# Gated MLP weights prepared during attention, one step per group, on one Trainium2 core

## The chip, the cores and the metric

The kernel runs on one core of a Trainium2 chip. The metric is the time of one execution on the device in microseconds (us), as the median of several runs. The core has a matrix engine (TensorE, PE in the rows; its weight loads are PEld), a vector engine (VectorE, DVE), a scalar engine (ScalarE, ACT), a general engine (GpSimd, POOL), an engine that issues the transfers here (SyncE, SP), and 16 DMA engines. The engines run their own instruction queues in order and wait for one another through semaphores.

## What is computed

Three layers follow one another: attention with pooled queries, a gated MLP with a spatial gate, and a mixer with a low-rank token part and a channel MLP.

```python
# 1 attention: q, k, v are (4, 8, 1152, 64)
q_pool = q.reshape(B, H, S // 2, 2, D).mean(axis=3)
attn = softmax(scale * q_pool @ k^T)          # 576 x 1152 for each of 32 heads
x = (attn @ v), heads side by side            # (4, 576, 512)
# 2 gated MLP
h = relu(x @ w_in);  u, v = halves of h       # w_in 512 x 1024
v_n = (v - mean) / sqrt(var + 1e-6)
gated = u * (w_spatial @ v_n + b_spatial)     # w_spatial 576 x 576
x = gated @ w_out                             # w_out 512 x 512
# 3 mixer
u = x + (x^T @ U @ V)^T                       # U 576 x 32, V 32 x 576
out = u + relu(u @ w_ch1) @ w_ch2
```

The weights w_in, w_out, U, V, w_ch1 and w_ch2 arrive as 64-bit floats; w_spatial, q, k, v arrive as 32-bit floats.

## The kernel before

**Attention** (`attention`) works on 16 pairs of heads, j = 0 to 15. Each pair has two halves of its 576 queries (256 and 320 wide, u = 2j and 2j + 1) and nine chunks of 128 keys, so 18 chunks a pair and 288 in all. Two chunks make a group: nine groups a pair (r = 0 to 8), 144 in all. In a group TensorE first runs up to two pieces (`piece`, a 128 x 384 block of scores whose row maximum VectorE reduces from PSUM, lines 138 and 142), then the two score products and the subtraction of the maxima (`scores`, `less`); ScalarE takes the exponentials (`expo`, line 197) into tiles `pt`; GpSimd adds up the exponentials (line 202); then come up to two more pieces and the products with v of the group before (`pv`). Pieces have two PSUM buffers (`ring`), so a piece waits for VectorE's reduction of the piece two earlier. In four of the nine groups of a pair VectorE also takes half a reciprocal (line 234, `waiting`).

**Weights** (class `Weights`): the 32-bit high and low parts that the matrix products use are made from each weight block (a unit) in seven phases, each one tick apart. For a 64-bit unit: phase 0, two ScalarE activations on the loaded words (lines 431, 432); phase 1 and phase 2, one VectorE instruction each (436, 438); phase 3, a GpSimd integer add (440); phase 4, VectorE (442); phase 5, the high part, by ScalarE or VectorE (452); phase 6, the low part, by GpSimd or VectorE (457). A 32-bit unit (w_spatial) has phases 5 and 6 alone. `tick` starts a unit when the one before it is at least two ticks old, and runs the due phase of up to four begun units. Loads go through three rooms `raw`; SyncE issues the next load when a room is free. The gated MLP has 21 units: 8 of w_in, 5 of w_spatial, 4 of w_out, 2 of U, 2 of V.

**The order of the gated MLP** (`gated_mlp`) is a generator that attention resumes through `also`. In the last two pairs (j = 14 and 15) attention resumes it after each chunk, and the table `TICKS` makes 13 ticks there; only the w_in units are loaded by then. The strings in `LEFT` interleave, at the end of attention, ticks (w), the split of batch 0's x (x) and batch 0's first products with w_in (v). Then the string `START` sets the order for batch 0: D finishes v (relu, statistics), n normalises, U makes the u half, b the bias, X splits batch 1's x, G the spatial gate, P the v products of batch 1, and w is a tick. The other 13 units are loaded and prepared in these ticks. After `START` come `y_part` (products with w_out), `u_pass` and `v_pass`, and then the batches 1 to 3 in a fixed loop without weight steps except for the channel MLP's in the last batch. The channel MLP (`channel_mlp`) follows.

Each engine's queue holds the instructions in the order in which this Python code issues them (`manual_schedule`).

Of the kernel before, what the change touches and what calls it, by code (L numbers as in the profile page):

```python
# [22 lines left out]
def f(ap):  # L23
    return ap.bitcast(F32)
# [3 lines left out]

LEFT = ("x x x x w x x v x x x v v w v", "v v v w v v w v v v v w", "v v v v w v v v w")


def attention(tc, idf, q, k, v, xs, also):

# [28 lines left out]
    with ExitStack() as ctx, ExitStack() as sco:  # L62
        pt_p = ctx.enter_context(tc.tile_pool(name="pt_p", bufs=12))
        ld2 = ctx.enter_context(tc.tile_pool(name="ld2", bufs=2))
# [10 lines left out]
        first = ld.tile([128, 128], F32R, name="first", bufs=1)  # L75
# [34 lines left out]
        def round_q(j, c0=0, c1=T):  # L110
            s = st[j]
            if "qr" not in s:
                s["qr"] = ld.tile([128, T], F32R, tag="qr", name="qr")
            nc.scalar.copy(s["qr"][:, c0:c1], s["q"][:, c0:c1])

        def round_k(j, c0=0, c1=S):
            s = st[j]
            if "kr" not in s:
                s["kr"] = ld.tile([128, S], F32R, tag="kr", name="kr")
            nc.scalar.copy(s["kr"][:, c0:c1], s["k"][:, c0:c1])  # L120
# [140 lines left out]
        pool_q(1, nc.gpsimd)  # L261
        ticks = [0]
        to_rows(0)
# [5 lines left out]
        for i, group in enumerate(groups):  # L269
# [36 lines left out]
            for u, n in waiting:  # L306
# [40 lines left out]
class Weights:  # L347
# [5 lines left out]
    def __init__(self, nc, stages, most=1 << 30, keep=None):  # L353
# [7 lines left out]
        self.time = self.begun = self.loaded = self.staged = 0  # L361

    def load(self, units=(), raws=()):

# [97 lines left out]
def gated_mlp(tc, idf, w_in, w_sp, b_sp, w_out, wU, wV, xs, us, last, soon, then):  # L462
# [4 lines left out]


    nc = tc.nc
    DM, DFF = w_in.shape  # L470
# [14 lines left out]

    right, mid, banks = ExitStack(), ExitStack(), ExitStack()
    ep = room(right, "ep", side="right")
    xn = ep.tile([128, KD, T], F32, name="xn")
    xnt = ep.tile([128, KD, TAIL], F32, name="xnt")

    wi = [None, ep.tile([128, 2, KD, FF], F32R, name="wi1")]
    raws = [ep.tile([128, 1024], F32, name=f"raw{i}") for i in range(3)]
# [18 lines left out]
    def load_x(b):  # L511
        nc.sync.dma_start(out=xn, in_=xs[b].rearrange("(k p) t -> p k t", p=128))
        if b % 2 == 0:
            nc.sync.dma_start(out=xnt, in_=xs[b + 1][:, 128 * (NT - 1):T].rearrange("(k p) t -> p k t", p=128))

    w = Weights(nc, stages, keep=LAST)
# [11 lines left out]
    wi[0] = e2.tile([128, 2, KD, FF], F32R, name="wi0")  # L528
    ps = [room(banks, "ps", 4, side="right", space=PSUM)]
# [60 lines left out]

    lp = room(last, "lp")
# [4 lines left out]
    uu = lp.tile([128, NT, 2, 2, R], F32R, name="uu")  # L596
    vv = lp.tile([128, 2, T], F32R, name="vv")
    yh = lp.tile([128, 2, NT, DM], F32R, name="yh")
    gg = lp.tile([128, DM], F32R, name="gg")
    wst = ap.tile([128, 2, NT, T], F32R, name="wst")  # L600
    wo = ap.tile([128, 2, KF, DM], F32R, name="wo")
# [3 lines left out]
    twice = lp.tile([128, TAIL], F32R, name="twice")  # L605

    first = ExitStack()
    sp = room(first, "sp")
    sps = [sp.tile([128, T], F32, name=f"sp{t}") for t in range(NT)]
# [4 lines left out]
    ES, EW, EU, EV = [engines(x) for x in ("ES", "EW", "EU", "EV")]  # L614
    units = []
    for t in range(NT):
        n = rows[t]
        units.append(
            ([(slice(p, p + n), w_sp[128 * t:128 * t + n]) for p in range(0, 128, n)], 128, (T,))
            + parts(nc, lambda t=t: [wst[:, 0, t]], lambda t=t, n=n: [wst[0:n, 1, t]], eng=ES[t][0], copy=ES[t][1], low=n)  # L620
            + (sps[t],)
        )
    for k in range(KF):
        units.append(
            ([(slice(None), w_out[128 * k:128 * k + 128])], 128, (DM,))
            + parts(nc, lambda k=k: [wo[:, 0, k]], lambda k=k: [wo[:, 1, k]], eng=EW[k][0], copy=EW[k][1])
        )
    full = 128 * (NT - 1)
    tail = wU[full:T].rearrange("(k p) r -> p k r", k=1)
    for src, k, sl in (  # L630
        ([(slice(None), wU[0:full].rearrange("(k p) r -> p k r", p=128))], NT - 1, slice(0, NT - 1)),
        ([(slice(p, p + TAIL), tail) for p in (0, TAIL)], 1, slice(NT - 1, NT)),
    ):
        units.append(
            (src, 128, (k, R))
            + parts(
                nc, lambda sl=sl: [uu[:, sl, i, 0] for i in range(2)],
                lambda sl=sl: [uu[:, sl, i, 1] for i in range(2)],
                lambda st: st.rearrange("p (k r) -> p k r", r=R), EU[k == 1][0], EU[k == 1][1],
            )  # L640
        )
    for h in range(2):
        sl = slice(HT * h, HT * h + HT)
        units.append(
            ([(slice(R * i, R * i + R), wV[:, sl]) for i in range(128 // R)], 128, (HT,))
            + parts(nc, lambda sl=sl: [vv[:, 0, sl]], lambda sl=sl: [vv[:, 1, sl]], None, *EV[h])
        )
    load_x(1)
    w.load(units)

    nc.gpsimd.memset(nhalf, -0.5)
    nc.gpsimd.memset(f(wst[64:128, 1, NT - 1]), 0.0)
    nc.gpsimd.memset(f(vn[64:128, 0, NT - 1]), 0.0)
# [253 lines left out]
LAST = 4  # L907
MORE = 4
# [1 line left out]
TICK = eval(os.environ.get('TK','[.9]*7'))  # L910

# [158 lines left out]
def tile_kernel(ctx: ExitStack, tc: tile.TileContext, q, k, v, w_in, w_sp, b_sp, w_out, wU, wV, w1, w2, out):  # L1070
# [9 lines left out]
    with tc.manual_schedule(), ExitStack() as last:  # L1080
        gated = gated_mlp(
            tc, idf, w_in, w_sp, b_sp, w_out, wU, wV, xs, us, last,
            lambda: next(channel), lambda: next(channel),
        )
        begun = []

        def also(i):
            if begun:
                try:
                    gated.send(i)  # L1090
                except StopIteration:
                    pass
            else:
                begun.append(next(gated))

        attention(tc, idf, q, k, v, xs, also)
        also(0)
        last.close()
        for _ in channel:
            pass  # L1100
# [42 lines left out]
```

## Time and profile before

| | us |
|---|---|
| median of 3 runs | 1237.76 (1237.42 to 1238.48) |
| the profiled execution's own time | 1240.44 |
| its span, first to last instruction | 1238.7 |
| TensorE busy | 1164.4 (94%) |
| VectorE busy | 646.3 (52%) |
| GpSimd busy | 559.9 (45%) |
| ScalarE busy | 438.2 (35%) |

The profile is of one execution. A busy TensorE is not TensorE at its peak, since the ends of its matmuls are modelled. The last exponentials of attention begin at 526.49 us; batch 1's u products begin at 640.22 us; the channel MLP's steady part runs from about 846 us to the end. The mean granted clock of TensorE over the span is 0.973 of full speed.

### The profile page before, as it was taken

How to read it: one execution, taken by the hardware profiler on the slowest of the kernel's cores; microseconds unless marked ns; L12 is line 12 of the kernel's file. 1: busy time of each engine (PE TensorE's matmuls, PEld its weight loads, DVE VectorE, ACT ScalarE, POOL GpSimd, SP SyncE). 2: the span in 40 equal slices, each digit the busy share in tenths (PEclk: the TensorE clock that was granted, in tenths of full speed). 3: DMA queues.
4: the chain of work that ended last, by engine and by line, in shares of the span. 5: the costliest groups of instructions: out<-in, count | busy, mean ns of one | idle time of the engine just before them, and what ended most of it. 6: DMA issues, size and time to landing. Idle time of an engine off the chain costs nothing.

```text
span 1238.7 us, 18191 instructions
## 1 busy us (share of the span) xinstructions
PE 1164.4 (94%) x7116; PEld 917.8 (74%) x7116; DVE 646.3 (52%) x1158; ACT 438.2 (35%) x868; POOL 559.9 (45%) x458
## 2 busy tenths in 40 slices
PE   7999999999999999887679999889999999999998
PEld 5666666666666665567569898768999999999997
DVE  4666666666666668865433332879862212121211
ACT  2444444444444445434233333646431111111110
POOL 2777777777777777953533343634420000000000
PEclk6999999999999999998889999989999999999999
DMA  6222222222222214141202001724310201010000
GB/s 153 62 68 68 66 65 64 59 69 66 65 66 63 67 39 140 61 140 46 67 9 69 26 22 42 222 103 154 122 58 1 77 1 52 1 51 1 26 1 26
DMA packets 37768, 79.17 MB, mean 64 GB/s; under 512 B 5553, under 2 KB 17841, under 8 KB 37682
## 3 DMA queue, kind: packets, MB, share of 16 engines
q1 hardware_dynamic: 37682, 78.01, 21.0%
q8 instruction: 56, 0.92, 0.3%
q14 instruction: 30, 0.25, 0.1%
HBM read 63.31 MB, written 14.16 MB: 63 GB/s over the span
## 4 chain that ended last, share of the span: by engine, by line
PE 44%; DVE 5%; DMA 3%; issue 1%; POOL 1%; ACT 1%; SPq 0%; POOLq 0%; ACTq 0%; DVEq 0%
PE ph L989 16%; PE py L1003 16%; PE pu L738 3%; PE py L786 3%; PE pg L756 2%; PE pv L557 2%; DVE st L442 1%; DVE w L457 1%; PE pt L981 1%; PE pV L811 1%; PE pU L772 1%; DVE st L436 1%; DMA raw<-in_moe_w_out_dram 1%; DMA sp<-in_moe_w_spatial_dram 0%; DMA un<-u 0%
## 5 line engine op out<-in xcount | busy, mean ns | idle before, releaser
L202 POOL TENSOR_TENSOR acc<-acc,pt 128x512 f32<-128x512 f32 (+1 forms) x222 | 315.6, 1422 | 105.6 <-ACT pt L197 94.3
L142 DVE TENSOR_REDUCE m<-r 128x1 f32<-128x384 f32 x480 | 249.3, 548 | 125.1 <-PE r L138 120.5
L197 ACT ACTIVATE pt<-s 128x512 f32<-128x512 f32 (+1 forms) x288 | 172.6, 648 | 248.7 <-PE s L186 205.1
L1003 PE MATMUL py<-w,h 128*128 128x512 f32 x864 | 217.2, 396 | 1.9 <-ACT h L992 1.7
L989 PE MATMUL ph<-ut,w 128*128 128x384 f32 x1152 | 218.0, 337 | 0.0
L989 PEld LDWEIGHTS ph<-ut,w 128*128 128x128 f32 x1152 | 204.9, 188 | 8.4
L993 DVE SCALAR_TENSOR_TENSOR h<-ph,h 128x384 fp32r<-128x384 f32 x96 | 53.5, 557 | 266.6 <-ACT h L992 266.6
L1003 PEld LDWEIGHTS py<-w,h 128*128 128x128 f32 x864 | 159.8, 188 | 32.4 <-ACT h L992 2.0
L177 PE MATMUL s<-q,k 64*128 64x320 f32 (+1 forms) x1152 | 177.6, 410 | 0.8 <-ACT pt L197 0.7
L213 PE MATMUL po<-pt,v 128*64 128x320 f32 (+1 forms) x1152 | 172.2, 420 | 0.0
L138 PE MATMUL r<-kr,qr 64*128 64x384 f32 x480 | 147.6, 428 | 15.8 <-DVE m L142 5.0
L992 ACT ACTIVATE h<-ph 128x384 fp32r<-128x384 f32 x96 | 47.2, 492 | 306.5 <-PE ph L989 306.5
L138 PEld LDWEIGHTS r<-kr,qr 64*128 64x128 f32 x480 | 72.7, 188 | 102.2 <-DVE m L142 63.3
L177 PEld LDWEIGHTS s<-q,k 64*128 64x128 f32 x1152 | 118.6, 188 | 12.8 <-ACT pt L197 3.1
L213 PEld LDWEIGHTS po<-pt,v 128*64 128x64 f32 x1152 | 70.1, 136 | 51.0 <-issue 22.3
L186 PE MATMUL s<-toprow,first 64*128 64x256 f32 (+1 forms) x576 | 102.1, 403 | 0.0
L440 POOL TENSOR_TENSOR st<-st,raw 128x512 int32<-128x512 int32 (+3 forms) x48 | 71.2, 1485 | 58.0 <-DVE st L438 40.7
L234 DVE RECIPROCAL sum<-sum 128x128 f32<-128x128 f32 (+1 forms) x64 | 66.8, 1046 | 36.0 <-ACT sum L229 36.0
L756 PE MATMUL pg<-wst,vn 128*128 128x288 f32 x448 | 65.0, 307 | 17.1 <-DVE ut L762 9.4
L756 PEld LDWEIGHTS pg<-wst,vn 128*128 128x128 f32 x448 | 63.4, 198 | 18.1 <-DVE ut L762 9.6
L186 PEld LDWEIGHTS s<-toprow,first 64*128 64x128 f32 x576 | 66.5, 189 | 10.7
L202 POOL TENSOR_TENSOR acc<-pt 128x512 f32<-128x512 f32 (+1 forms) x32 | 45.3, 1415 | 22.0 <-ACT pt L197 20.6
(117 smaller groups left out, 1141.5 us busy)
## 6 DMA issues: line engine op xcount, KB each, us to landing
raw<-in_moe_w_ch_dram SPq DMA_DIRECT2D x32, 512.0 KB, 3.7
k<-in_k_dram SPq DMA_DIRECT2D x32, 288.0 KB, 4.5
qraw<-in_q_dram SPq DMA_DIRECT2D x32, 288.0 KB, 5.7
v<-in_v_dram SPq DMA_DIRECT2D x16, 576.0 KB, 4.2
xn<-x SPq DMA_DIRECT2D x4, 1152.0 KB, 5.7
out_dram<-un SPq DMA_DIRECT2D x18, 256.0 KB, 2.1
raw<-in_moe_w_in_dram SPq DMA_DIRECT2D x8, 512.0 KB, 3.7
u<-o SPq DMA_DIRECT2D x16, 256.0 KB, 2.0
```

The source lines that it names most:

```text
L138: nc.tensor.matmul(r, s["qr"][p, q0:q0 + 128], s["kr"][p, PW * i:PW * i + PW], start=True, stop=True)
L142: nc.vector.tensor_reduce(out=m[:, e, i:i + 1], in_=r, axis=AX.X, op=ALU.max, negate=True)
L177: nc.tensor.matmul(t[:, e, 0:n], s["k"][p, 128 * c:128 * c + 128], s["q"][p, q0:q0 + n], start=True, stop=False)
L186: nc.tensor.matmul(jb["s", c][:, e, 0:n], first[p], jb["top"][p, 0:n], start=False, stop=True)
L197: nc.scalar.activation(x[:, :, 0:n], t[:, :, 0:n], ACTF.Exp, scale=SC)
L202: nc.gpsimd.tensor_tensor(out=a, in0=jb["p", 0][:, :, 0:n] if c == 1 else a, in1=x[:, :, 0:n], op=ALU.add)
L213: nc.tensor.matmul(jb["o"][D * e:D * e + D, 0:n], st[u // 2]["v"][:, e, c], x[:, e, 0:n], start=c == 0, stop=c == KC - 1,)
L234: nc.vector.reciprocal(out=t, in_=t)
L440: nc.gpsimd.tensor_tensor(out=o, in0=o, in1=lo, op=ALU.add)
L756: nc.tensor.matmul(p[:, 0:HT], vn[:, a, s, 128 * m:128 * m + 128], wst[:, c, s, sl], start=s == 0 and i == 0, stop=s == NT - 1 and i == 1,)
L989: nc.tensor.matmul(p[:, 0:BT], w1s[m][:, a, k], ut[i][:, c, k], start=j == 0, stop=j == 3 * KD - 1)
L1003: nc.tensor.matmul(py[i][c], h[:, a, 128 * c:128 * c + 128], w2s[m][:, e], start=m == 0 and a + e == 0, stop=m == KM - 1 and a == 1,)
```

## The change

All 21 units of the gated MLP are put into one list. Attention resumes the generator once in every group (`also(i)`, after the group's products with v and its sums), instead of after every chunk of the last two pairs. From group 8 on, each call makes one tick, and `apart` (new) lets a unit begin six ticks after the one before it, so that only phase 0 of a unit shares a tick with phase 6 of the one before. The last unit's phase 6 falls on group 134 of 144. The load of batch 0's x moves to group 100. `LEFT`, `START` have no w any more, and the order of the other letters changes: in `START` all U come before all X, all X before all G, all G before all P. `w_in`'s and `w_spatial`'s rooms are now open during attention. To make room, `pt` has 8 buffers instead of 12, the five separate w_spatial rooms `sp` go (w_spatial uses the rooms `raw`), and attention's `idr`, `first`, `tops` and the rounded copies of k and q lie in slices of the tile `yh`, which the gated MLP uses later.

```diff
-LEFT = ("x x x x w x x v x x x v v w v", "v v v w v v w v v v v w", "v v v v w v v v w")
+LEFT = ("x x x x v v v v", "x x v v v v x x x", "v v v v v v v v v")
-def attention(tc, idf, q, k, v, xs, also):
+def attention(tc, idf, q, k, v, xs, rounded, also):
-        pt_p = ctx.enter_context(tc.tile_pool(name="pt_p", bufs=12))
+        pt_p = ctx.enter_context(tc.tile_pool(name="pt_p", bufs=8))
+        def carve(n):
+            used[0] += n
+            return rounded[:, used[0] - n:used[0]]
-        idr = ld.tile([128, 128], F32R, name="idr", bufs=1)
+        idr = carve(128)
-        tops = [[ld.tile([128, 128], F32R, name=f"top{i}{c}", bufs=1) for c in range(5)] for i in range(2)]
+        tops = [[carve(128) for c in range(5)] for i in range(2)]
+        krs = [carve(S) for _ in range(2)]
+        qrs = [carve(T) for _ in range(2)]
...
             for u, c in group:
                 less(u, c)
                 expo(u, c)
-                if j >= NP - 2:
-                    also(ticks[0])
-                    ticks[0] += 1
...
             waiting = [(u, n + 1) for u, n in waiting if n < 2] + [(u, 0) for u, c in group if c == KC - 1]
+            also(i)
...
+        self.apart = 2
-            if i < self.loaded and (i == 0 or self.time - self.units[i - 1]["begun"] > 1):
+            if i < self.loaded and (i == 0 or self.time - self.units[i - 1]["begun"] >= self.apart):
...
-    w = Weights(nc, stages, keep=LAST)
-    w.load(w_in_units(1) + w_in_units(0), raws)
-    load_x(0)
+    LAST = len(units) - 1
+    w = Weights(nc, stages, keep=LAST)
+    w.apart = 6
+    yield yh.rearrange("p a t d -> p (a t d)")
+    nc.gpsimd.memset(f(wst[64:128, 1, NT - 1]), 0.0)
     i = 0
     while not isinstance(i, str):
-        w.tick(CFG["TICKS"].get(i, 0))
+        if i == WEIGHTS:
+            w.load(units, raws)
+        if i >= WEIGHTS:
+            w.tick()
+        if i == X_AT:
+            load_x(0)
         i = yield
+    w.end()
+    w.apart = 2
...
-    TICKS={i: 1 for i in range(4, 30, 2)},
-    START="w v v w v v v w D v w D D v w w D w D w U w U n w U w U U n n n w U n b w U n U U w U U U U U w U w "
-    "U U U X n X X X U X X w w U X G G U X w G X X w w w G G w G G w w w G G w w G G G G G G G G P P w w "
-    "P P P w w P w w w w w P w w P w w P w P w w w w w",
+    START="D D D D U D U n U n U n U n U n U n U n b U U U U U U U U U " + "X " * 9 + "G " * 17 + "P " * 9,
+WEIGHTS = 8
+X_AT = 100
```

Line numbers in the changed kernel are 8 to 20 higher: the reduction of a piece is L151 there (L142 before), the weight phases L439 to L465 (L431 to L457 before).

VectorE's queue in the middle of attention, around a pair's first 128-wide reciprocal. `m<-r` is the reduction of a piece, `sum` the softmax sums, `x` the head's output, `st`, `raw` and `wi` belong to the weights. Before:

```order
L142 TENSOR_REDUCE m<-r 128x1 x6
L145 TENSOR_REDUCE top_105<-m 128x2
L234 RECIPROCAL sum<-sum 128x128
L142 TENSOR_REDUCE m<-r 128x1 x3
L234 RECIPROCAL sum<-sum 128x128
L240 TENSOR_TENSOR x<-po,sum 128x256
```

Now:

```order
L151 TENSOR_REDUCE m<-r 128x1 x6
L154 TENSOR_REDUCE yh<-m 128x2
L243 RECIPROCAL sum<-sum 128x128
L450 SCALAR_TENSOR_TENSOR st_99<-raw_97,st_99 128x512
L151 TENSOR_REDUCE m<-r 128x1 x3
L243 RECIPROCAL sum<-sum 128x128
L249 TENSOR_TENSOR x<-po,sum 128x256
L460 CAST wi_93<-st_99 128x512
```

A phase of a weight unit stands behind each reciprocal, ahead of the next group's reductions; there was none in this part of the program.

ScalarE's queue in batch 0, from the last relus of the u half (`ut<-pu`) into the spatial gate (`gt<-ut`, `gtt<-ut`); `xt<-xn` is the split of batch 1's x, `raw`, `st` and `wo` belong to the weights. Before:

```order
L744 ACTIVATE ut<-pu 128x288 x3
L431 ACTIVATE st_4964<-raw_4959 128x512
L432 ACTIVATE raw_4959<-raw_4959 128x512
L452 CAST wo<-st_4962 128x512
L744 ACTIVATE ut<-pu 128x288
L338 CAST xt<-xn 128x576 x3
L431 ACTIVATE st_4965<-raw_4961 128x512
L432 ACTIVATE raw_4961<-raw_4961 128x512
L338 CAST gt<-ut 128x288
L338 CAST xt<-xn 128x576
```

Now:

```order
L344 CAST wst<-bb 1x576
L764 ACTIVATE ut<-pu 128x288 x4
L344 CAST xt<-xn 128x576 x4
L344 CAST gt<-ut 128x288
L344 CAST gt<-ut 128x224
L344 CAST gtt<-ut 128x64
```

The weight activations that read a loaded block (`raw`) stood between the gate's splits; in this stretch there are none now.

## Rows read from the trace of the kernel before

**Rows 1.** Windows: stretch, length, busy PE, PEld, DVE, ACT, POOL, clock, DMA share, GB/s.

```profile
212.57:243.93 31.36, 30.38 (x229) 19.84 (x227) 20.68 (x42) 14.07 (x27) 23.93 (x18) 1.00 0.22 62
526.49:551.13 24.64, 20.62 (x91) 13.84 (x89) 16.62 (x27) 9.16 (x18) 14.34 (x15) 0.93 0.27 91
551.13:640.22 89.09, 62.74 (x323) 54.68 (x322) 45.92 (x81) 32.32 (x73) 40.83 (x46) 0.83 0.21 63
```

**Rows 2.** Timeline of ScalarE, exponentials that open a group: start, us, instruction, wait.

```profile
212.57 1.09 ACT L197 ACTIVATE pt<-s 128x512 f32<-128x512 f32 x2 [1.57 <-PE s L186]
...
219.87 0.60 ACT L197 ACTIVATE pt<-s 128x512 f32<-128x512 f32 x1 [0.53 <-PE s L186]
...
243.93 0.60 ACT L197 ACTIVATE pt<-s 128x512 f32<-128x512 f32 x1 [1.58 <-PE s L186]
...
463.35 0.60 ACT L197 ACTIVATE pt<-s 128x512 f32<-128x512 f32 x1 [1.57 <-PE s L186]
...
497.25 1.08 ACT L197 ACTIVATE pt<-s 128x512 f32<-128x512 f32 x2 [1.58 <-PE s L186]
...
507.39 0.60 ACT L197 ACTIVATE pt<-s 128x512 f32<-128x512 f32 x1 [1.51 <-PE s L186]
```

**Rows 3.** Groups by line, 526 to 641 us: busy, mean ns, idle before, releasers.

```profile
L756 PE MATMUL pg<-wst,vn 128*128 128x288 f32 x112 | 20.0, 344 | 17.1 <-DVE ut L762 9.4 <-DVE wst L457 6.7 <-ACT vn L338 1.0
...
L431 ACT ACTIVATE st<-raw 128x512 f32<-128x512 f32 (+3 forms) x9 | 4.8, 536 | 40.5 <-DMA raw<-in_moe_w_out_dram 14.3 <-DMA raw<-in_moe_V_dram 9.3 <-DMA raw<-in_moe_U_dram 8.6
L557 PE MATMUL pv<-wi,xtt 128*128 128x512 f32 x12 | 4.6, 552 | 2.8 <-ACT v L695 2.8
L772 PE MATMUL pU<-yh,uu 128*128 128x512 f32 x8 | 3.4, 495 | 8.1 <-ACT yh L338 8.1
```

**Rows 4.** Timeline of TensorE, 540 to 600 us: batch 0's u products.

```profile
551.13 12.98 PE L738 MATMUL pu<-xt,wi 128*128 128x288 f32 x96
```

**Rows 5.** Chain that ended last, 630 to 760 us, in order of time: start, us, what.

```profile
656.28 14.85 PE pg L756 x112
...
684.76 5.59 PE py L786 x24
...
699.67 3.18 PE pu L738 x24
...
730.58 10.90 PE pv L557 x48
```

**Rows 6.** Groups of VectorE by line and shape, 474 to 507.4 us: weight phases.

```profile
L442 DVE SCALAR_TENSOR_TENSOR st<-raw,st 128x512 int32<-128x512 int32 x3 | 4.7, 1582 | 0.0
L438 DVE TENSOR_SCALAR st<-st 128x512 int32<-128x512 int32 x4 | 4.1, 1032 | 0.0
L436 DVE TENSOR_SCALAR st<-st 128x512 f32<-128x512 f32 x4 | 2.3, 566 | 0.0
...
L452 DVE CAST wi<-st 128x512 fp32r<-128x512 f32 x1 | 1.8, 1773 | 0.0
...
L457 DVE TENSOR_TENSOR wi<-st,wi 128x512 fp32r<-128x512 f32 x1 | 0.7, 678 | 0.0
```

**Rows 7.** Timelines of VectorE, GpSimd and TensorE in steady attention, 225 to 238 us.

```profile
226.15 1.02 DVE L142 TENSOR_REDUCE m<-r 128x1 f32<-128x384 f32 x2 [2.00 <-PE r L138]
...
235.94 0.95 DVE L234 RECIPROCAL sum<-sum 128x128 f32<-128x128 f32 x1 [1.33 <-ACT sum L229]
236.81 1.59 DVE L142 TENSOR_REDUCE m<-r 128x1 f32<-128x384 f32 x3
...
232.80 4.82 POOL L202 TENSOR_TENSOR acc<-acc,pt 128x640 f32<-128x640 f32 x3
...
237.43 0.37 PE L138 MATMUL r<-kr,qr 64*128 64x384 f32 x1
```

**Rows 8.** DMA issues by line: KB each, median us from issue to landing.

```profile
raw<-in_moe_w_in_dram SPq DMA_DIRECT2D x8, 512.0 KB, 3.7
```

More of the change, by code (lines that the diff above doesn't have):

```diff
@@ L73, in attention @@
         nc.gpsimd.memset(ones, 1.0)
-        first = ld.tile([128, 128], F32R, name="first", bufs=1)
+        first = carve(128)
         nc.gpsimd.memset(f(first), 0.0)
-        tops = [[ld.tile([128, 128], F32R, name=f"top{i}{c}", bufs=1) for c in range(5)] for i in range(2)]
+        tops = [[carve(128) for c in range(5)] for i in range(2)]
         for t in tops[0] + tops[1]:
             nc.gpsimd.memset(f(t), 0.0)
+        krs = [carve(S) for _ in range(2)]
+        qrs = [carve(T) for _ in range(2)]
         for e in range(2):
@@ L112, in round_q @@
             if "qr" not in s:
-                s["qr"] = ld.tile([128, T], F32R, tag="qr", name="qr")
+                s["qr"] = qrs[j % 2]
             nc.scalar.copy(s["qr"][:, c0:c1], s["q"][:, c0:c1])
@@ L118, in round_k @@
             if "kr" not in s:
[L119 removed]
+                s["kr"] = krs[j % 2]
             nc.scalar.copy(s["kr"][:, c0:c1], s["k"][:, c0:c1])
@@ L261, in attention @@
         pool_q(1, nc.gpsimd)
-        ticks = [0]
         to_rows(0)
@@ L486, in gated_mlp @@
     right, mid, banks = ExitStack(), ExitStack(), ExitStack()
+    lp = room(last, "lp")
+    uu = lp.tile([128, NT, 2, 2, R], F32R, name="uu")
+    vv = lp.tile([128, 2, T], F32R, name="vv")
+    yh = lp.tile([128, 2, NT, DM], F32R, name="yh")
+    gg = lp.tile([128, DM], F32R, name="gg")
+    twice = lp.tile([128, TAIL], F32R, name="twice")
+    wp = room(mid, "wp")
+    wst = wp.tile([128, 2, NT, T], F32R, name="wst")
+    wo = wp.tile([128, 2, KF, DM], F32R, name="wo")
     ep = room(right, "ep", side="right")
@@ L489, in gated_mlp @@
     xnt = ep.tile([128, KD, TAIL], F32, name="xnt")
-    wi = [None, ep.tile([128, 2, KD, FF], F32R, name="wi1")]
+    wi = [ep.tile([128, 2, KD, FF], F32R, name=f"wi{h}") for h in range(2)]
     raws = [ep.tile([128, 1024], F32, name=f"raw{i}") for i in range(3)]
@@ L514, in load_x, with w_sp_units @@
             nc.sync.dma_start(out=xnt, in_=xs[b + 1][:, 128 * (NT - 1):T].rearrange("(k p) t -> p k t", p=128))
+    ES, EW, EU, EV = [engines(x) for x in ("ES", "EW", "EU", "EV")]
+    def w_sp_units():
+        for t in range(NT):
+            n = rows[t]
+            yield (
+                ([(slice(p, p + n), w_sp[128 * t:128 * t + n]) for p in range(0, 128, n)], 128, (T,))
+                + parts(
+                    nc, lambda t=t: [wst[:, 0, t]], lambda t=t, n=n: [wst[0:n, 1, t]],
+                    eng=ES[t][0], copy=ES[t][1], low=n,
+                )
+            )
@@ new lines, in gated_mlp @@
+    units = w_in_units(1) + w_in_units(0) + list(w_sp_units())
+    for k in range(KF):
+        units.append(
+            ([(slice(None), w_out[128 * k:128 * k + 128])], 128, (DM,))
+            + parts(nc, lambda k=k: [wo[:, 0, k]], lambda k=k: [wo[:, 1, k]], eng=EW[k][0], copy=EW[k][1])
+        )
+    full = 128 * (NT - 1)
+    tail = wU[full:T].rearrange("(k p) r -> p k r", k=1)
+    for src, k, sl in (
+        ([(slice(None), wU[0:full].rearrange("(k p) r -> p k r", p=128))], NT - 1, slice(0, NT - 1)),
+        ([(slice(p, p + TAIL), tail) for p in (0, TAIL)], 1, slice(NT - 1, NT)),
+    ):
+        units.append(
+            (src, 128, (k, R))
+            + parts(
+                nc, lambda sl=sl: [uu[:, sl, i, 0] for i in range(2)],
+                lambda sl=sl: [uu[:, sl, i, 1] for i in range(2)],
+                lambda st: st.rearrange("p (k r) -> p k r", r=R), EU[k == 1][0], EU[k == 1][1],
+            )
+        )
@@ L516, in gated_mlp @@
+    for h in range(2):
+        sl = slice(HT * h, HT * h + HT)
+        units.append(
+            ([(slice(R * i, R * i + R), wV[:, sl]) for i in range(128 // R)], 128, (HT,))
+            + parts(nc, lambda sl=sl: [vv[:, 0, sl]], lambda sl=sl: [vv[:, 1, sl]], None, *EV[h])
+        )
+    LAST = len(units) - 1
     w = Weights(nc, stages, keep=LAST)
-    w.load(w_in_units(1) + w_in_units(0), raws)
-    load_x(0)
+    w.apart = 6
+    yield yh.rearrange("p a t d -> p (a t d)")
+    nc.gpsimd.memset(f(wst[64:128, 1, NT - 1]), 0.0)
@@ L589, in gated_mlp @@
         i = yield
-    lp = room(last, "lp")
     lps = room(last, "lps", 2, space=PSUM)
@@ L604, in gated_mlp @@
     nhalf = ap.tile([128, 1], F32, name="nhalf")
-    twice = lp.tile([128, TAIL], F32R, name="twice")
     first = ExitStack()
     sp = room(first, "sp")
-    sps = [sp.tile([128, T], F32, name=f"sp{t}") for t in range(NT)]
     bb = sp.tile([128, T], F32, name="bb")
@@ L613, in gated_mlp @@
     V0 = [e for e, _ in engines("V0")]
[L614 to L647, printed above, removed]
     load_x(1)
-    w.load(units)
     nc.gpsimd.memset(nhalf, -0.5)
-    nc.gpsimd.memset(f(wst[64:128, 1, NT - 1]), 0.0)
     nc.gpsimd.memset(f(vn[64:128, 0, NT - 1]), 0.0)
@@ L1084, in tile_kernel @@
         )
-        begun = []
+        rounded = next(gated)
+        next(gated)
         def also(i):
[L1088 to L1096, printed above, removed]
+            try:
+                gated.send(i)
+            except StopIteration:
+                pass
+        attention(tc, idf, q, k, v, xs, rounded, also)
         also(0)
```

11 lines of the change are left out of this document (1 added, 10 removed).

## The prediction

> **What bounds the kernel now.** I read the windows first. In steady attention (first row of [rows 1]) a pair of heads takes 31.36 us, and TensorE is busy for 30.38 of them: attention is bound by TensorE. The other engines have room there: VectorE is busy for 20.68, GpSimd for 23.93, ScalarE for 14.07. The stretch from batch 0's u products to batch 1's (third row of [rows 1]) is another picture: 89.09 us, of which TensorE is busy for 62.74, at a granted clock of 0.83 of the 2.4 GHz level. The groups by line say what ended TensorE's idle time there [rows 3]: the spatial gate (L756) stood for 17.1 us, most of it for VectorE's gate product and for a low part of w_spatial; the U products (L772) stood 8.1 us for ScalarE's split of y. ScalarE itself had stood 40.5 us at the first weight phase, most of it for loads of w_out, V and U. Its queue is in order, so the gate's and y's splits stood behind phases whose data had not landed. So this stretch is bound by the preparation of the weights, and all its other work waits in the same queues.
>
> The chain shows what the same work takes where no weights are in the way [rows 4, 5]: u 12.98 us, gate 14.85, v of the next batch 10.90 (48 matmuls), y 14.91 (from 684.76 to 699.67).
>
> **The change part by part.** The sum is made on the profiled execution, 1240.44 us, and is moved by -2.7 us at the end, which is what the median of 1237.76 lies below it.
>
> 1. Removed: 13 of the 21 units leave the stretch from 551.13 to 640.22. TensorE's work there is then u + gate + v + y = 12.98 + 14.85 + 10.90 + 14.91 = 53.64 us at the full clock, against 89.09: 35.4 less if nothing waits. What is late next is batch 0's own normalisation: five statistics on VectorE and GpSimd, an exchange of halves through two DMAs, splits on three engines, all due by the gate's start; the u products' 13 us cover it, just. I take 2.5 us of waits there. In the tail of attention (second row of [rows 1]) TensorE is idle for 4.0 of 24.64 us, 2.8 of it before the last v products, for a relu that stood on ScalarE behind a weight copy (L557 in [rows 3]); I take 3 us of that as saved. Together -36 us. The bounds: -39.4 if no wait is left (35.4 + 4.0), and -26 if TensorE's busy time stays at 62.74, the low clock with it.
>
> 2. Removed: the ticks in pairs 14 and 15. Pair 14 took 497.25 - 463.35 = 33.90 us, 2.54 more than the steady pair; the first two groups of pair 15 took 10.14 us, where those of a steady pair take 7.30 [rows 2], 2.84 more. Together -5.4 us. Nothing replaces them, since the last phase now falls on group 134, in pair 14.
>
> 3. Added: all 21 units in groups 8 to 134. Phases 1, 2 and 4 of 16 units are 48 VectorE instructions; eight of the 21 high parts and seven of the low parts are VectorE's too: 63, of which 15 belong to the small units of U and V. The nearest price is the one that attention paid in the part above: between 474 and 507.4 us VectorE ran 13 weight phases there, 13.6 us busy, 1.05 us each [rows 6], and attention lost 5.4 us, 0.41 us for each. With the 15 small ones at half, 55.5 x 0.41 = 23 us. The bounds are far apart: nothing, since VectorE is idle for 10.7 us of a steady pair and about 4.5 instructions come in each; and 63 x 1.05 = 66 us, if TensorE waits for every one to its full length. I stay at 23 for two reasons that pull apart. A third of the places hide a phase: VectorE waits 2.00 us for the next piece ahead of 226.15 [rows 7]. But the groups with a reciprocal hide nothing: it starts at 235.94 and takes 0.95 us, the next reductions follow without a gap, TensorE's piece at 237.43 needs the first of them, and the changed order puts a phase between. GpSimd's adds are running there until 237.62 [rows 7].
>
> How much a phase is lengthened by GpSimd is seen in rows 6: L436 and L438 are of one kind and size, and took 566 and 1032 ns. The Trainium skill, SBUF — State Buffer, "Who interferes with whom", says that VectorE in its two-port mode, or with two SBUF inputs, and GpSimd exclude each other, and the second to come waits until the first has finished. The trace agrees as far as these two means go. That rule speaks against this change: it moves the phases to where GpSimd is busy for three quarters of the time; what it makes of the time is the third rival.
>
> ScalarE's phases (two activations and a copy or none) lie in groups with about 1.6 us of idle time ahead of the exponentials [rows 2], and GpSimd's 30 instructions (16 adds, 14 low parts, two in a pair) fit into the 7.4 us that it idles in a pair [rows 1]; I cost both at nothing. If that cover were gone, GpSimd would delay the sums. The buffers of `pt` (8, four groups' worth) cost nothing as long as GpSimd runs no more than about three groups behind.
>
> 4. Added: in group 8 the first unit's load and its phase 0 come in one tick. ScalarE then stands for the landing, 3.7 us after the issue [rows 8], and the exponentials stand behind it. SyncE runs ahead by about a group, so part is covered: 1.5 us, between 0 and 3.7. The later loads are issued 14 groups ahead of their use, about 48 us, and the k, q and v loads behind them on SyncE's queue are a pair or two ahead. The memory sharing adds no instruction; the one memset that moves to the start (w_spatial's tail) is at most half a microsecond on GpSimd while the first k and q load, and counts as nothing.
>
> Sum: -36 - 5.4 + 23 + 1.5 = -16.9. 1240.4 - 16.9 = 1223.5 on the profiled execution, 1221 us as a median.
>
> **The rivals.**
>
> - The phases hide (chance 0.15). Attention pays only in the groups with a reciprocal, some 10 us. For it: one instruction a group where there were two or three, and 2 us gaps in some groups. Against it: TensorE has only 1 us idle in a pair to give. Time 1221 - 13 = 1208.
> - Batch 0 is bound by its own normalisation (0.15). The chain from the last v products over statistics, the exchange and the splits ends later than u, or the clock falls in the wait. For it: it was never seen without weights for batch 0, and batch 0 has no y ahead of its gate to cover it, as the later ones have. Then -26 instead of -36: 1231.
> - TensorE inherits nearly every phase, slower (0.10). The place is steady attention: each phase waits for the add that GpSimd has begun, the reductions stand behind it and the next piece behind them. If two thirds of the places pay their full 1.05 us and the lost time of GpSimd brings the others to half, 63 x 0.9 = 57 us instead of 23: 1255. It decides from (36 + 5.4 - 1.5) / 63 = 0.63 us a phase; 0.41 was measured. By the Trainium skill's rule taken alone (SBUF — State Buffer, "Who interferes with whom"), each phase can cost up to a whole add (4.82 / 3 = 1.6 us [rows 7]) plus its own time, which would be this case.
> - GpSimd falls behind in the 320-wide halves (0.06), where its adds already run one behind the other [rows 7], and the sums of each pair wait 1 us for them: 15 us more, 1236, within 0.2% of before.
> - The change doesn't do what it says, in that phases still meet loads that have not landed: not likely with loads 14 groups ahead (0.02, about the time before).
>
> **How the numbers follow.** The forecast has 0.52, the rivals 0.15, 0.15, 0.10, 0.06 and 0.02. Predicted is 1221 us. The range holds the forecast with attention paying 10 to 35 us (1208 to 1233) and the first two rivals; the end at 1237 leaves out the slower case, the end at 1207 a full hiding with no wait left in batch 0. About 0.2% (2.5 us) is what a measurement of this kernel can tell from no change: faster 0.84, same 0.06, slower 0.10.
>
> **What would show each step.** The steady pair of the changed kernel, by the starts of the exponentials: 31.36 + 23 / 14 = 33.0 us on average, and the groups with a reciprocal longest; at 31.5 the phases hide, above 34.2 attention costs more than it frees. From batch 0's u products to batch 1's: 56 us, clock near 1.0 throughout; over 62 the second rival holds. Pair 15 back to about 26 us with no weight phase in it. No idle time of ScalarE for a weight load but the first. The prediction is wrong if VectorE's weight phases delay TensorE by a price other than 0.4 us, since that is the one large term without a row in the same place.

## The result, and the profile after

The changed kernel takes 1220.93 us as a median (1220.57 to 1226.0), the kernel before, run beside it, 1238.12 us (1237.42 to 1239.76): a ratio of 0.9869, with a 95% interval of 0.9841 to 0.9896. The forecast was 1221 us. The profiled execution took 1220.57 us where 1223.5 was forecast for it, and 1240.44 us before: 19.9 us less.

The windows of the changed kernel follow: stretch, length, busy PE, PEld, DVE, ACT, POOL, clock, DMA share, GB/s. The first is from attention's first exponentials to those that open pair 15, the second pair 14, the third the tail from attention's last exponentials on, the fourth from batch 0's u products to batch 1's.

```profile
22.72:522.87 500.15, 468.45 (x3401) 300.16 (x3398) 362.39 (x682) 232.93 (x451) 396.14 (x285) 0.99 0.28 77
488.50:522.87 34.37, 31.38 (x230) 19.90 (x227) 25.44 (x48) 15.13 (x31) 24.14 (x18) 1.00 0.09 27
548.19:567.26 19.07, 18.91 (x92) 13.02 (x91) 10.00 (x21) 7.09 (x14) 4.45 (x8) 1.00 0.21 69
567.26:620.65 53.39, 53.39 (x322) 48.59 (x322) 22.38 (x45) 22.07 (x47) 20.44 (x26) 1.00 0.11 32
```

The fourth row answers to the third of [rows 1]: 89.09 us has become 53.39, TensorE is busy for all of it, at the full clock, and DVE and POOL are busy for half as long, ACT for two thirds. The first row is to be held against this one of the kernel before, where pair 14 still held weight ticks:

```profile
22.92:497.25 474.33, 456.95 (x3400) 298.90 (x3397) 317.90 (x624) 215.62 (x413) 360.17 (x256) 0.99 0.24 67
```

The third row answers to the second of [rows 1]: 24.64 us has become 19.07.

The chain that ended last has nothing but TensorE in batch 0 (start us, us, what):

```profile
567.26 12.71 PE pu L758 x96
579.97 14.85 PE pg L776 x112
594.83 10.91 PE pv L623 x48
605.73 5.59 PE py L806 x24
...
620.65 3.18 PE pu L758 x24
```

Each piece begins where the one before ends. They are the lengths that [rows 4] and [rows 5] had given for the same products. The spatial gate, for which TensorE stood 17.1 us in [rows 3], makes it wait for nothing now (groups by line, 546 to 621 us: busy, mean ns, idle before):

```profile
L776 PE MATMUL pg<-wst,vn 128*128 128x288 f32 x112 | 15.0, 295 | 0.0
```

Put together from the starts of the exponentials and of the u products, the two profiled executions differ like this (us; the first column of times is the kernel before):

| stretch | before | after | difference |
|---|---|---|---|
| start to first exponentials | 22.92 | 22.72 | -0.2 |
| first exponentials to pair 15 | 474.33 | 500.15 | +25.8 |
| pair 15 to the last exponentials | 29.24 | 25.32 | -3.9 |
| tail, to batch 0's u products | 24.64 | 18.91 | -5.7 |
| batch 0, to batch 1's u products | 88.93 | 53.39 | -35.5 |
| the rest | 598.6 | 598.3 | -0.3 |

(The tail and batch 0 go here by the first u product seen in the trace; the windows above by the piece that contains it.) Pair 14 before held 2.5 us of weight ticks, which are gone too, so the steps that moved into attention cost 25.8 + 2.5 = 28.4 us with rounding. By the windows, 14.3 of the 25.8 us are idle time of TensorE and 11.5 are longer busy time; since the ends of its matmuls are modelled, that split is rough.

### The profile page after: what moved, and what is told of

Read it like the earlier page. It is cut to its first block, busy times and chain, and to the rows that moved or that the text cites. A ratio compares the mean times of both kernels' runs of the same rounds, so it can differ in the third digit from the quotient of the medians.

```text
span 1218.8 us, 18185 instructions
## 1 busy us (share of the span) xinstructions
PE 1164.7 (96%) x7116; PEld 912.9 (75%) x7116; DVE 646.3 (53%) x1158; ACT 438.8 (36%) x868; POOL 558.3 (46%) x458
## 4 chain that ended last, share of the span: by engine, by line
PE 50%; DVE 4%; DMA 0%; ACT 0%; issue 0%; POOL 0%; ACTq 0%; DVEq 0%
PE ph L1006 16%; PE py L1020 16%; PE pu L758 4%; PE pv L623 4%; PE pg L776 4%; PE py L806 3%; DVE w L465 1%; DVE st L450 1%; PE pV L831 1%; PE pt L998 1%; PE pU L792 1%; DVE st L444 1%; DVE st L446 0%; DMA raw<-in_moe_w_ch_dram 0%; DVE yh L345 0%
## 5 line engine op out<-in xcount | busy, mean ns | idle before, releaser
L151 DVE TENSOR_REDUCE m<-r 128x1 f32<-128x384 f32 x480 | 250.3, 550 | 103.1 <-PE r L147 98.0
L147 PE MATMUL r<-yh 64*128 64x384 f32 x480 | 149.5, 431 | 21.3 <-DVE m L151 11.8
L147 PEld LDWEIGHTS r<-yh 64*128 64x128 f32 x480 | 70.9, 188 | 113.0 <-DVE m L151 73.7
L195 PE MATMUL s<-toprow,yh 64*128 64x256 f32 (+1 forms) x576 | 100.7, 405 | 0.0
L195 PEld LDWEIGHTS s<-toprow,yh 64*128 64x128 f32 x576 | 64.6, 190 | 11.7 <-issue 0.4
L776 PE MATMUL pg<-wst,vn 128*128 128x288 f32 x448 | 60.1, 295 | 0.0
L776 PEld LDWEIGHTS pg<-wst,vn 128*128 128x128 f32 x448 | 59.6, 188 | 0.0
```

The lines of the kernel that those rows point to most:

```text
L147: nc.tensor.matmul(r, s["qr"][p, q0:q0 + 128], s["kr"][p, PW * i:PW * i + PW], start=True, stop=True)
L151: nc.vector.tensor_reduce(out=m[:, e, i:i + 1], in_=r, axis=AX.X, op=ALU.max, negate=True)
L195: nc.tensor.matmul(jb["s", c][:, e, 0:n], first[p], jb["top"][p, 0:n], start=False, stop=True)
L776: nc.tensor.matmul(p[:, 0:HT], vn[:, a, s, 128 * m:128 * m + 128], wst[:, c, s, sl], start=s == 0 and i == 0, stop=s == NT - 1 and i == 1,)
```

## The experiments

All stretches below are from the first exponentials to pair 15, unless another is named; 471.8 us is what the kernel before takes for it without its 2.5 us of ticks in pair 14.

**Is the order of batch 0 the gain, or that the weights have left it?** The old strings are put back, with the weights still in attention:

```diff
-LEFT = ("x x x x v v v v", "x x v v v v x x x", "v v v v v v v v v")
+LEFT = ("x x x x w x x v x x x v v w v", "v v v w v v w v v v v w", "v v v v w v v v w")
-    START="D D D D U D U n U n U n U n U n U n U n b U U U U U U U U U " + "X " * 9 + "G " * 17 + "P " * 9,
+    START="w v v w v v v w D v w D D v w w D w D w U w U n w U w U U n n n w U n b w U n U U w U U U U U w U w "
...
```

> The changed kernel with the two order strings of before (LEFT and START); the ticks in them find no work left. Tells what part of the gain at batch 0 is the weights' leaving and what part the new order. Theory: the weights' leaving is nearly all; from batch 0's u products to batch 1's 54 to 57 us (53.4 in the changed kernel, 89.1 before), time 1221 to 1225. Rival: the old order interleaves u, gate and x so that it waits by itself; then 62 us or more and a time of 1229 or more.

Measured: 1219.4 us (1218.98 to 1221.43), ratio to before 0.9832 (0.9813 to 0.985). Its window from batch 0's u products to batch 1's:

```profile
565.30:618.69 53.39, 53.39 (x321) 48.59 (x320) 24.70 (x53) 21.92 (x48) 22.11 (x29) 1.00 0.17 53
```

The same 53.39 us without a gap, just below the expected 54 to 57. The new order adds nothing; that the weights have left is the whole gain.

**Were the landings what held batch 0, or the phases' own work?** The kernel before, with the loads of w_out, U and V left out and their phases kept:

```diff
-            for r, src in u["src"]:
+            for r, src in u["src"] if "own" in u or not self.stale else ():
...
     load_x(1)
+    w.stale = True
     w.load(units)
```

> The kernel before, with the loads of w_out, U and V of the gated MLP left out: their weight phases all stay where they were, behind the last groups and in batch 0, and work on what the rooms still hold of w_in, so ScalarE meets no load there but w_spatial's. (w_out, U and V are thus not the reference's.) It splits the 35.7 us that batch 0 gave back. Theory, as the prediction had it, that the landings were the larger part (ScalarE stood 32.2 us for these loads): from batch 0's u products to batch 1's 60 to 72 us where it was 89, and 1210 to 1223 us. Rival, that the phases' own work in the in-order queues, among the gate's and y's splits, is what took the time, and that the landings were only what came last: 80 to 89 us, and 1230 to 1240 us.

Measured: 1219.88 us (one run; before beside it 1239.89). Batch 0's window, and what ScalarE waited for from 548 to 620 us (in total, times, longest):

```profile
548.76:620.04 71.28, 59.94 (x322) 52.34 (x320) 46.69 (x81) 32.07 (x73) 41.39 (x46) 0.88 0.13 39
```

```profile
ACT vn L338 <- DVE v L674: 18.7, 6, 4.1
ACT yh L338 <- PE py L788: 6.6, 3, 3.2
ACT gt L338 <- DVE ut L764: 6.2, 2, 4.6
ACT wst L453 <- DMA sp<-in_moe_w_spatial_dram: 4.7, 1, 4.7
```

The stretch falls by 17.8 of the 35.7 us that the change took away. The landings of these three weights were half; the other half stays when no load but w_spatial's is waited for, with the clock at 0.88. That is within what the theory expected, at its edge, but "the larger part" is not shown. What is left is seen in TensorE's own waits in this run (549 to 620 us: in total, times, longest):

```profile
PE pg L758 <- DVE wst L458: 6.7, 2, 4.5
PE pU L774 <- ACT yh L338: 3.4, 1, 3.4
```

The 9.4 us for the gate product in [rows 3] are gone and the 8.1 us for y's split are 3.4, but the 6.7 us for w_spatial's low part stand as they did. So of the 17.9 us that are left, 11.3 are idle time of TensorE (71.28 less 59.94), most of it for that low part, and 6.6 are longer busy time (59.94 for 53.39), with the lower clock. Whether the low part comes late by w_spatial's load or by its place in the queues is not shown.

**What do the steps in attention cost, and which of them?** Three kernels leave one kind out or put a stand-in there. Without VectorE's phases 1, 2 and 4 (48 of VectorE's 63 instructions; the weights are then not made):

```diff
-            if phase == 1:
+            if phase in self.left:
+                pass
+            elif phase == 1:
...
+    w.left = (1, 2, 4)
```

> The changed kernel without the VectorE phases 1, 2 and 4 of the gated MLP's 16 64-bit units (48 instructions; the weights are then not the true ones). Theory: attention lost 28 us to the weight steps because VectorE's phases delay its reductions, about 0.43 us each; without 48 of 63 some 20 us come back, the first exponentials to those of pair 15 take about 479 us instead of 500.2, the time is about 1201 us. Rival: attention is slower because of GpSimd's and ScalarE's phases or because of the shared rooms and 8 instead of 12 buffers; then 495 us or more and a time of 1216 or more.

Without GpSimd's phase 3 (`w.left = (3,)` in the same edit):

> The changed kernel without phase 3, the 16 GpSimd adds of the gated MLP's units (weights not the true ones). Theory: GpSimd has room and its adds cost little by themselves; attention takes 495 to 499 us instead of 500.2, only where VectorE's phase 4 waited for such an add (some 1.2 us in each of four groups), time 1216 to 1220. Rival: GpSimd's share of the weight steps is what attention pays for; then 485 us or less and a time below 1208.

And with phases 1, 2 and 4 replaced by a VectorE instruction that reads one input of the same size and writes one element a row:

```diff
-            if phase == 1:
+            if self.spare is not None and phase in (1, 2, 4):
+                nc.vector.tensor_reduce(out=self.spare[0:u["p"]], in_=st, axis=AX.X, op=ALU.max)
+            elif phase == 1:
```

> The changed kernel with the VectorE phases 1, 2 and 4 of the gated MLP's units replaced by a maximum over the same 512 elements, written to one element (one SBUF input; weights not the true ones). As many VectorE instructions stand at the same places in its queue. If what costs is that the phases are drawn out while a GpSimd add runs, the stand-ins take 0.6 us each with no spread, and attention takes 485 to 492 us instead of 500.2, time about 1206 to 1213. If the mere place in the queue costs, attention stays at 497 or more and the time at 1218 or more.

Measured: 1203.19, 1218.58 and 1211.58 us (one run each; before beside them 1240.32). The windows of the three in that order, one kernel a fence:

```profile
22.78:504.62 481.84, 461.24 (x3401) 299.56 (x3398) 324.61 (x634) 232.92 (x450) 389.45 (x285) 0.99 0.29 79
```

```profile
22.59:520.54 497.95, 466.01 (x3401) 299.35 (x3398) 356.34 (x682) 233.20 (x450) 380.91 (x270) 0.99 0.28 77
```

```profile
22.53:513.33 490.80, 466.02 (x3401) 300.24 (x3398) 346.84 (x682) 232.64 (x451) 389.47 (x285) 0.99 0.28 78
```

Against 500.15 us: VectorE's 48 phases cost 18.3 us, GpSimd's adds of phase 3 cost 2.2 us, and the stand-ins, equal in number and place, cost 9.4 us less than the real phases. Why they cost less is in the groups of VectorE by line and shape (busy, mean ns, idle before). The changed kernel, 30 to 522 us:

```profile
L450 DVE SCALAR_TENSOR_TENSOR st<-raw,st 128x512 int32<-128x512 int32 x12 | 16.6, 1384 | 2.4 <-POOL st L448 2.4
L446 DVE TENSOR_SCALAR st<-st 128x512 int32<-128x512 int32 x12 | 8.0, 669 | 0.0
L444 DVE TENSOR_SCALAR st<-st 128x512 f32<-128x512 f32 x12 | 7.9, 662 | 0.4 <-ACT st L439 0.4
```

The stand-ins, 30 to 512 us:

```profile
L445 DVE TENSOR_REDUCE spare<-st 128x1 f32<-128x512 f32 x36 | 23.8, 662 | 2.4 <-POOL st L451 2.0 <-ACT st L440 0.4
```

All 36 stand-ins took between 0.63 and 0.69 us, whatever GpSimd did. L446 took 0.36 us in some places and up to 1.43 in others, L450 0.63 and up to 1.75. One long one, in the changed kernel's timeline of GpSimd, VectorE and TensorE (start, us, instruction, wait):

```profile
155.86 1.31 POOL L448 TENSOR_TENSOR st<-st,raw 128x512 int32<-128x512 int32 x1
157.12 1.28 POOL L211 TENSOR_TENSOR acc<-pt 128x512 f32<-128x512 f32 x1
...
157.21 1.75 DVE L450 SCALAR_TENSOR_TENSOR st<-raw,st 128x512 int32<-128x512 int32 x1 [0.60 <-POOL st L448]
...
158.88 1.63 DVE L151 TENSOR_REDUCE m<-r 128x1 f32<-128x384 f32 x3
...
159.47 0.91 PE L147 MATMUL r<-yh 64*128 64x384 f32 x2 [0.76 <-DVE m L151]
```

Phase 4 waits for GpSimd's integer add, and when that ends, GpSimd's next add begins 0.09 us ahead of it. Phase 4 ends 0.56 us after that add, which is a little less than the 0.63 us that it takes undisturbed. The reductions stand behind it, and TensorE's piece behind these: the gap to the next exponentials is 1.2 us longer than before, once in each of four units. In the kernel without phase 3 these four gaps are as before; of the 4.9 us, 2.7 come back at other places, which is why only 2.2 are left for phase 3. The Trainium skill, SBUF — State Buffer, "Who interferes with whom", has the rule: whichever of the two engines issues first holds the shared ports for its whole instruction, and the other stands still; a reduction with one input is left alone. The trace agrees with both halves, by the rows above.

**VectorE's splits.** All high parts go to ScalarE and all low parts to GpSimd; nothing is left out:

```diff
-    EI="pa vv va pv va pv pa pa",
-    ES="va pa pa vv va",
+    EI="pa pa pa pa pa pa pa pa",
+    ES="pa pa pa pa pa",
...
```

> The changed kernel with all 21 high parts on ScalarE and all low parts on GpSimd, so 15 VectorE instructions less in attention and 15 more on engines that have room. Theory: at 0.43 us each, 4 to 6 us less: 1215 to 1217. Rival: GpSimd, with 7 more operations of 1.3 us, falls behind in the 320-wide halves and gives it back: 1220 or more.

Measured: 1213.88 us (1212.54 to 1216.48), ratio to before 0.9787 (0.9763 to 0.9812).

```profile
22.96:515.56 492.60, 465.68 (x3401) 299.93 (x3398) 349.77 (x666) 236.55 (x459) 401.38 (x292) 1.00 0.28 78
```

Another 7.5 us back for 15 instructions, 0.5 us each, where 4 to 6 us were expected and 1215 to 1217 us; the same work on ScalarE and GpSimd shows no price of that size.

**The buffers of `pt`.** The kernel before, with `bufs=8` for `bufs=12` as its only edit:

> The kernel before with 8 instead of 12 buffers for the exponentials, nothing else. Theory: no exponential waits for a buffer, so no change: 1238 us within 1 us. Rival: the smaller buffer is part of what attention lost in the changed kernel: 1241 us or more.

Measured: 1239.05 us (1237.27 to 1242.68), ratio 0.9993 (0.9981 to 1.0005). No cost, as the prediction had it. This is without the weights in attention; with them no run has 12 buffers, and the only bound is the version with chosen places below, which has 8 and lies 4.7 us above the kernel with no weights there.

**Does the place in the pair matter?** First by shifting all units by one group or two (`WEIGHTS = 7`, then 6), which moves every phase to another place in the pair's nine groups:

> The changed kernel with the first tick in group 7 instead of 8, so each phase falls on the neighbouring place in a pair: phase 4 moves from r = 0, 3, 6 to r = 2, 5, 8. Theory: the place decides what a phase costs; phase 4 at r = 0 (1.2 us four times) and the phases at r = 6 (0.3 to 1.4 us) go, others come at r = 2; attention takes 492 to 497 us instead of 500.2, time 1214 to 1218. Rival: every VectorE phase costs the same wherever it stands: 500 us and 1221 within 1 us.

> The changed kernel with the first tick in group 6: phase 4 at r = 1, 4, 7, phases 1 at 7, 1, 4 and 2 at 8, 2, 5. Theory: by the costs read at those places, phase 4 behind the reciprocal at r = 1 is dear, the others cheaper; attention 497 to 502 us, time 1218 to 1223. Rival (place does not matter): 1221 within 1 us. This run and the one from group 7 are judged together: different times speak for the place.

Measured: from group 7 on 1233.85 us (1230.3 to 1238.71), ratio to before 0.995 (0.9927 to 0.9972), where a gain on the changed kernel was expected: a miss with the wrong sign. From group 6 on 1217.39 us (1215.52 to 1218.82), ratio 0.9812 (0.9792 to 0.9831), just below the expected 1218 to 1223; its attention, 497.82 us, is in the expected range. The kernel that begins in group 7, in an execution of 1238.44 us, one of the two longest of its seven:

```profile
22.42:540.57 518.15, 477.71 (x3401) 308.48 (x3398) 368.42 (x682) 232.52 (x451) 394.60 (x286) 0.96 0.27 74
```

That is 18 us more than in the changed kernel; for 9 of them TensorE is busy for longer, with the clock at 0.96. Behind the low clock of the start, which both kernels have, it has eight stretches of 3.4 to 6.8 us at half the clock (a granted clock of 0.50) within attention. The changed kernel has one, and there one sees what came ahead of it (windows, then the timeline of VectorE and TensorE):

```profile
166.50:170.80 4.30, 2.95 (x27) 2.00 (x25) 3.15 (x7) 1.68 (x5) 3.41 (x3) 1.00 0.11 38
170.80:174.20 3.40, 3.40 (x18) 2.29 (x18) 1.38 (x3) 0.87 (x2) 0.18 (x2) 0.50 0.00 0
```

```profile
166.18 1.03 PE L186 MATMUL s<-q,k 64*128 64x256 f32 x8
...
167.07 0.84 DVE L465 TENSOR_TENSOR wi<-st,wi 128x512 fp32r<-128x512 f32 x1
...
168.43 0.29 PE L168 MATMUL tr<-yh 64*128 64x64 f32 x1 [0.99 <-DVE m L151]
...
170.88 2.12 PE L186 MATMUL s<-q,k 64*128 64x256 f32 x8
```

A low part stands ahead of the reduction that the transposes (L168) wait for. TensorE stands 0.99 us, then for part of the transposes too; after a stretch in which it was busy for 2.95 of 4.30 us the granted clock is at half, and the same eight score products take 2.12 us for 1.03. The group is 1.9 us longer than before. The wait alone does not settle it: in the kernel without phase 3 the same low part takes 0.85 us at the same place and TensorE stands 0.98 us, but the clock stays at 1.00 and the group is 0.8 us longer. What decides between the two is not shown. In the kernel from group 7 on, it is phase 4 that stands at this place, in five units, and a stretch at half the clock follows in four of them. Once, in its timeline and the window behind it:

```profile
141.50 0.84 DVE L450 SCALAR_TENSOR_TENSOR st<-raw,st 128x512 int32<-128x512 int32 x1
...
142.86 0.29 PE L168 MATMUL tr<-yh 64*128 64x64 f32 x1 [0.98 <-DVE m L151]
```

```profile
144.10:147.50 3.40, 3.40 (x16) 2.06 (x16) 1.02 (x3) 0.35 (x3) 1.17 (x1) 0.50 0.32 118
```

The place does matter, then, and the shift by one had moved phases to a worse one.

**The places chosen.** From the gaps between the exponentials of the changed kernel, pair by pair, I took where each phase costs little, gave the fifteen large units (the expectation says sixteen) starts nine groups apart, at the last group of a pair, so that phases 1, 2 and 4 always stand at the first, second and fourth group of the nine, and put w_spatial's five units and a small one in between; the splits are off VectorE as above. Nothing is left out:

```diff
+    wide = [i for i in range(LAST + 1) if not 2 * KD <= i < 2 * KD + NT]
+    small = wide.pop(-3)
+    for n, i in enumerate(wide):
+        order.append(i)
+        starts.append(9 * n)
+        if n in (2, 4, 6, 8, 10):
+            order.append(2 * KD + n // 2 - 1)
+            starts.append(9 * n + 3)
...
```

> The changed kernel with every high part on ScalarE and every low part on GpSimd, and with the sixteen large units begun at the first group of a pair's nine each, so that VectorE's phases (three a unit) always stand at that pair's first, second and fourth group; the five units of w_spatial and the one small unit of U go in between. Nothing is left out. Theory, by the prices that the places showed in the changed kernel (about 0 for the first phase in the first group, 0.4 for one in the second, 0.4 or nothing for one in the fourth): the groups from the first exponentials to pair 15 take 476 to 481 us and the time is 1199 to 1204 us. Rival, that a phase of VectorE costs its 0.45 us wherever it stands, so that the place is worth nothing and only the number counts: 490 to 494 us and 1212 to 1215 us, as the version with all splits off VectorE had.

> The same, with the second VectorE phase of each unit put into the same group as the first, the first of the pair's nine. Theory, that this group has VectorE time to spare and the second has not: another 3 to 7 us less in attention than with the phases one a group, 472 to 477 us, and a time of 1195 to 1200 us. Rival, that two phases in a row outlast the room of one group: 4 us or more above the one-a-group version.

Measured: one phase a group 1199.12 us (1197.34 to 1201.9), ratio to before 0.9671 (0.9649 to 0.9694). With phase 2 in the same group as phase 1, 1205.92 us (1202.61 to 1209.03), ratio 0.9723 (0.9698 to 0.9747). The first kernel's window, then the second's:

```profile
22.81:499.34 476.53, 456.48 (x3401) 297.86 (x3398) 342.98 (x663) 236.14 (x458) 401.11 (x291) 1.00 0.29 80
```

```profile
22.40:509.08 486.68, 466.19 (x3401) 300.11 (x3398) 356.57 (x663) 236.26 (x458) 402.29 (x291) 0.99 0.28 79
```

The number of VectorE's phases is that of the version with the splits off VectorE; by their places, with the order and spacing of the units that go with them, attention falls by 16.1 us, to 4.7 above the kernel with no weights in it (the medians differ by 14.8; three of the phases now fall in pair 15, behind this window, where pair and tail are 0.5 us longer). Once the first units are loaded, a large unit costs 0.33 us, about the length of its phase 2, in the third gap of a pair, and nothing elsewhere. The second kernel's expectation failed and its rival held: a pair in the middle of attention takes 32.1 to 32.2 us, where the first kernel takes 31.7. Why is seen in the same phase 2 at its two places; first by group (20 to 500 us), then in the timeline. One phase a group:

```profile
L449 DVE TENSOR_SCALAR st<-st 128x512 int32<-128x512 int32 x12 | 4.4, 363 | 0.0
```

Two in one group:

```profile
L449 DVE TENSOR_SCALAR st<-st 128x512 int32<-128x512 int32 x12 | 16.3, 1356 | 0.4
```

```profile
155.45 1.58 POOL L468 TENSOR_TENSOR wst<-raw,wst 128x576 fp32r<-128x576 f32 x1
155.81 1.51 DVE L449 TENSOR_SCALAR st<-st 128x512 int32<-128x512 int32 x1
...
157.24 0.55 DVE L151 TENSOR_REDUCE m<-r 128x1 f32<-128x384 f32 x1
```

A group later GpSimd is idle when phase 2 comes, and it takes 0.36 us. Right behind phase 1 it meets an instruction that GpSimd began 0.36 us earlier, and ends 0.29 us after that one's end; so it does in eleven of the twelve large units of this shape.

## Why the prediction was right, point by point

**Batch 0 and the tail** were forecast at -36 us, with bounds of -26 and -39.4, and gave -41.2, outside the bounds. The 35.4 us by the chain's lengths were right (35.5 measured). Two smaller terms were not. The 2.5 us of waits for batch 0's own normalisation do not exist: TensorE is busy for 53.39 of 53.39 us. In the tail I allowed at most the 4.0 us of idle time, while 5.7 went: TensorE's busy time there fell too, from 20.62 to 18.91 us, as the clock rose from 0.93 to 1.00. I had counted the low clock in batch 0 and not in the tail, though both rows of [rows 1] show it. The second rival, that batch 0 is bound by its own normalisation, fell with these waits.

**The ticks of pairs 14 and 15** were forecast at -5.4 us; pair 15 gave 3.9 and pair 14's 2.5 make it -6.5.

**VectorE's phases in attention** were forecast at 0.41 us each. The runs give 18.3 us for the 48 phases and 7.5 for the 15 splits, 25.8 / 63 = 0.41 us on average, if the two add up, which no run tried. The price was right, the sum of 23 us was not: I had taken 15 instructions of the small units at half, and these were not cheaper (from group 110 on, where they stand, the gaps between the exponentials are 7.7 us longer than before, 0.5 us for each). As an explanation the price was only half right. It is a mean over places that cost 0 and places that cost 1.2 us and more, and the reciprocals alone do not tell them apart. The pairs from the second to the fifteenth take 33.3 us on average (33.0 forecast), 27.3 us more in all, of which 19.2 lie in the gaps that follow a group with a reciprocal and the rest elsewhere. Groups with one hide nothing, that was right: phase 2 right behind a 160-wide reciprocal takes 0.36 us and costs 0.33. But a group without one hides nothing either when phase 4 meets an add there and costs 1.2. By the stand-ins and the chosen places, what tells the places apart is whether GpSimd is in an add when the phase begins, and whether a reduction that TensorE waits for stands right behind it.

**GpSimd's steps** were costed at nothing; the sixteen adds cost 2.2 us, by when phase 4 can begin and what it then meets. Its low parts and ScalarE's phases were left out in no run. The rival that GpSimd falls behind did not come true: none of TensorE's waits in attention ends with one of its adds (23 to 548 us), and seven more operations on it went with a gain.

**The first load** was forecast at 1.5 us. ScalarE stood 2.4 us for it (waits of the changed kernel, 30 to 621 us):

```profile
ACT st L439 <- DMA raw<-in_moe_w_in_dram: 2.4, 1, 2.4
```

The gap there is 2.0 us longer and the next two are 1.5 us shorter, so that about 0.5 us is left. No other load of a weight was waited for, as forecast. The memset that moves to the start takes 0.58 us, a little over the half microsecond forecast, and the start is no longer for it.

**The sum** was -16.9 us for the profiled execution and is -19.9. Attention with the first load came out 3.9 us dearer than forecast (28.4 for 24.5), batch 0, the tail and the ticks 6.3 better. The further 2.7 us that I took off for the median were not there, since the profiled execution after, 1220.57 us, lies at its median; that made up for the 3 us. That 1221 was met to 0.1 us is thus luck, errors that cancel; the signs of the two large terms and their sizes to some 5 us are what was right.

**The rivals.** That TensorE inherits nearly every phase needed 0.63 us each; it was 0.41. By the rule of the Trainium skill alone (SBUF — State Buffer, "Who interferes with whom") it would have come so; the rule describes each meeting rightly, but only some of the phases meet an add, and where VectorE has time to spare a meeting costs nothing: at the pair's fourth group phase 4 still takes up to 1.75 us in the version with chosen places, and no gap is longer for it. That the phases hide (1208 us) did not come true for the change as it stands; the version with chosen places shows that they can. What stays open is why, with the landings gone, batch 0 still waits 6.7 us for w_spatial's low part, and which of its waits bring the clock down.

## What to carry to other kernels

In this kernel, preparation work that delayed a stretch in which TensorE waited was worth moving under a stretch that TensorE bounds, even at a price per step there. But the price is a matter of place: of the 28 us that these steps cost, 24 came back by choosing for each phase a group in which VectorE has time ahead of the reduction that TensorE waits for, and by keeping a short one away from GpSimd's adds, with the splits on other engines. A shift of the whole plan by one group, without looking, cost some 10 us (0.995 for 0.9869 of the kernel before).

## What the runs showed of the hardware

- The same VectorE instruction on the same data, 128x512 by a constant, takes 0.36 us where GpSimd is idle and 1.36 us on average at a place where, in eleven of twelve units, GpSimd had begun an instruction 0.35 us before; a one-input reduction of the same size takes 0.63 to 0.69 us in either case.
- A wait of TensorE of 0.99 us ahead of some small transposes was followed by 3.4 us at a granted clock of 0.50, so that a low part of 0.84 us made a group 1.9 us longer; in the kernel without phase 3 a wait of 0.98 us at the same place was not, and the group was 0.8 us longer.
